# A write of ones moved behind the last causal masks of batch 0, and two copies of a transposed head moved from VectorE to ScalarE

## Chip, cores and metric

The kernel runs on one core of one Trainium2 chip. The metric is the device time of one execution in microseconds (us); of the kernel before there are three timed runs and one profiled execution. Engines go by the names of the profile: PE is TensorE (PEld its weight loads), DVE is VectorE, ACT is ScalarE, POOL is GpSimd, SP is SyncE, which here only issues DMAs.

## What is computed

Attention with a causal mask and a bias made of cumulative sums, over 8 batches of 8 heads (576 tokens, head size 64), then a mixer: a low-rank product over the tokens and a two-layer network over the 512 channels.

```python
s_pos = np.maximum(s, 0.0)
cum = np.cumsum(s_pos, axis=-1)
bias = -(cum[:, :, :, None] - cum[:, :, None, :])
scores = np.where(causal, -1e9, scale * q @ k.T + np.minimum(bias, 0.0))
attn = softmax(scores)
x = (attn @ v).transpose(0, 2, 1, 3).reshape(B, S, H * D)
u = x + (x.transpose(0, 2, 1) @ U @ V).transpose(0, 2, 1)
out = u + np.maximum(u @ w_ch1, 0.0) @ w_ch2
```

(`k.T` stands for the last two axes exchanged.)

## The kernel before

Heads are worked on in pairs: pair n = 4b + hp holds heads 2hp and 2hp + 1 of batch b, `hh` says which of the two. One pair passes through these steps:

- T(n), `transposes` (from L310): PE turns q and k so that the head size lies along the partitions (L325), for each `hh` into one PSUM bank `pwork`. Two copies for each `hh` (L348; `par` 0 and 1, even and odd tokens) bring them into the pair's `slot` in SBUF. `copies` (L296) says which engine copies: VectorE or ScalarE.
- The slot has four more rows (64 to 67) for the bias: `rows_of` (L303) brings two DMAs of cumulative sums from HBM, queued on SP; the other halves of these rows are ones. Slots 0 to 3 have their ones from batch 0's own rows. Slot 4, `slots[PB]`, first used by pair 4, gets them from the memset of L1169.
- S(n), `scores` (from L439): four steps, each a few matmuls (L443) into PSUM and an exponential on ScalarE into the tile `pT`: one for head 0 and one for head 1 (L461), one for the middle blocks of both (L473, "S6 mid" below for pair 6), and one for the last 64 tokens (L479, "S6 tail"), whose matmuls write a bank `pwork`. In batch 0 the causal masks are three `affine_select` instructions on GpSimd for each pair (`masks`, L391, by way of L158): head 0, head 1, and the last 64 tokens of both. From batch 1 on VectorE masks (L387).
- V(n), `values` (from L495): for each `hh` 15 matmuls (L507) into a bank `pwork`, then a reciprocal (L516) and a multiplication (L517) on VectorE, which frees the bank.

There are four banks `pwork`, given out and taken back as they fall free, and two double banks `pscore`. Around batch 0's end stand `mix_first` (M0 to M3, L621; its first half has the products of L625, its second those of L632 and L640 and a copy on ScalarE, L648) and the first blocks of the channel network's first layer, `hidden_first` (L677), which need the first half of `w_ch1` (`load_w1(0)`, 1 MB, issued by POOL at L1154). The second layer of batch 0's tokens starts with `ahead[0]` and `ahead[1]`: two banks `pwork`, begun by L688 and L696.

What sets the order: PE and POOL run in the order of the program (L1332), and up to L1205 DVE, ACT and SP do too. Behind that line a planner, which works with estimated durations, sets the order on DVE, ACT and SP, and which bank a tile gets. The order of steps is written out by hand. At batch 0's end on POOL it is: masks of pair 2, a small memset (L1167), the load of the second half of `w_ch1` (L1168), the memset of L1169, the masks of pair 3 (L1176), loads of q and k of batch 1 (L1177), of half of `w_ch2` (L1178). PE meanwhile goes S3, V1, M0, S3, V2, M0, M1, V3, M1, M2. In batch 1 the words around the moved copies are "S6 T7 S6 T7 S6 S6" and then "V4 V4 S7 V5" (L1247, L1248), with pieces of the channel network between them.

From batch 3 on, q and k are turned by DMA: `load_pair` loads a pair, `turn_pair` (L364) queues a DMA transpose on SP behind the last turned output of V (L524), and `part_pair` (L373) copies the result into the slot on VectorE (L377). `seqmix` (L531) mixes the tokens of a finished batch and begins with products over all its `x_sb` (L537).

Of the kernel before, what the change touches and what calls it, by code (L numbers as in the profile page):

```python
# [41 lines left out]
def kernel(  # L42
# [12 lines left out]
    nc = tc.nc  # L55
    traced = len(nc.cur_bb.bb.instructions)
    E = mybir.EngineType
    B, H, S, D = q.shape
# [8 lines left out]
    PB = NP // B  # L67
    TP, TT = 72, 8
    NG = B * S // 512
    KA = D + 4  # L70
# [46 lines left out]
    def in_runs(b, h):  # L117
        return b > 2 or b == 2 and h >= 4
# [10 lines left out]
    def load_qk(b, h, n):  # L129
        for dst, src in ((q_t[b], q), (k_t[b], k)):  # L130
            if in_runs(b, h):
                nc.gpsimd.dma_start(
                    out=dst[:, ds(h, n), :].rearrange("p h (t d) -> p (h t) d", t=TT),
                    in_=src[b, ds(h, n)].rearrange("h (t p) d -> p (h t) d", p=TP),
                )
            else:
                nc.gpsimd.dma_start(
                    out=dst[:, ds(h, n), :],
                    in_=src[b, ds(h, n)].rearrange("h (p t) d -> p h (t d)", p=TP),
                )  # L140
# [58 lines left out]
    slots = [consts.tile([128, 2, S + SK], BF16, name=f"slot{i}") for i in range(NSLOT)]  # L199
# [66 lines left out]
    def load_w1(half):  # L266
        nc.gpsimd.dma_start(
            out=w1_sb[:, :, ds(half * 1024, 1024)], in_=w1_in[:, :, ds(half * 1024, 1024)]
        )

    def load_w2(half):
        nc.gpsimd.dma_start(
            out=w2_sb[:, ds(half * 8, 8), :],
            in_=moe_w_ch2[ds(half * 1024, 1024)].rearrange("(kt kp) n -> kp kt n", kp=128),
        )
# [19 lines left out]

    def copies(n, hh, par):  # L296
        b = n // PB
        on_act = hh == (n == 4) and (
            n in (0, 4, 8, 9) or (n, par) == (1, 0) or n > 8 and n % PB == 2
        )  # L300
        return nc.scalar.copy if on_act else nc.vector.tensor_copy

# [7 lines left out]
    def transposes(n):  # L310
# [24 lines left out]
        for hh in range(2):  # L335
            if b > 0:
                turn(hh, 0)
            turn(hh, 1)
            tp = tps[hh]
            dst = slot[0:D, hh, 0 : 2 * S]  # L340
            for par in range(2):
                src = tp[par * D : par * D + D]
                if in_runs(b, 2 * hp):
                    by_run = dst.rearrange("p (c t two m) -> p c t two m", c=2, t=4, two=2)
                    copies(n, hh, par)(by_run[:, :, :, par, :], src)
                else:
                    in_turn = dst.rearrange("p (c m t two) -> p c m t two", c=2, t=4, two=2)
                    copies(n, hh, par)(  # L348
                        in_turn[:, :, :, :, par], src.rearrange("p c t m -> p c m t")
                    )  # L350
            yield
# [31 lines left out]
    def mask(dst, n_tiles, w, on_pool=False):  # L383
        if on_pool:
            causal(dst, n_tiles, w)
        else:
            nc.vector.tensor_tensor(  # L387
                dst, dst, keep[:, :, 0:w].to_broadcast([128, n_tiles, w]), op=ALU.min
            )

    def masks(pT, on_pool):  # L391
        for hh in range(2):
            mask(pT[:, hh, 0:512].rearrange("p (a b) -> p a b", a=4), 4, 128, on_pool)
        mask(pT[:, :, 1536:1600], 2, 64, on_pool)
# [726 lines left out]
    def pT_of(n):  # L1121
        if n < PB + 3:
            return pTs[n % 2] if n % PB < 2 else pT_early[n % PB - 2]
        return pTs[(n + 1) % 2]

    def step(*gens):
        for gen in gens:
            next(gen, None)
# [37 lines left out]
    masks(pT_of(2), True)  # L1166
    nc.gpsimd.memset(pT_early[1][:, :, 1600:], 1.0)  # L1167
    load_w1(1)  # L1168
    nc.gpsimd.memset(slots[PB][D:KA, :, 0 : 2 * S].bitcast(mybir.dt.uint32), 0x3F803F80)  # L1169
    step(S3)  # L1170
    step(V1)
    step(S3)
# [1 line left out]
    step(M0)  # L1174
    step(S3, S3)
    masks(pT_of(3), True)  # L1176
    load_qk(1, 4, 4)  # L1177
    load_w2(0)  # L1178
    nc.gpsimd.memset(V_end, 0.0)
# [183 lines left out]
```

## Time and profile before

| | |
|---|---|
| timed runs | 351.04 us median of 3 (350.96 to 352.51) |
| profiled execution | 351.77 us, of which the span of instructions is 349.9 us |
| granted TensorE clock | 1.00 |
| PE busy | 96% of the span |
| DVE, ACT, POOL busy | 75%, 59%, 34% |
| chain that ended last, by engine | PE 66%, DVE 12%, DMA 7%, POOL 6%, issue 4%, ACT 3% |
| idle time of PE in the list of its waits, 13 rows | 7.3 us |

The span is what the profile shows of the instructions; the rest of a run's time lies around it. The profile's lists of waits name for each engine whom it waited for, how long in total, how often, and the longest. A timeline line has start, duration, engine, line, operation, output<-input and form; "x3" means three merged instructions, and brackets hold the idle time before and what ended it. PE is busy nearly all the time, so a removed wait of PE can show in the end, if no later wait takes it back.

### The profile page before, as it was taken

To read this page: it belongs to the slowest core of one execution; us is meant where nothing else is said; L and a number is where in the kernel's file an instruction comes from. 1 tells how busy PE (TensorE), PEld (TensorE's weight loads), DVE (VectorE), ACT (ScalarE), POOL (GpSimd) and SP (SyncE) were. 2 spreads that over 40 slices of the span, in tenths; PEclk is the share of its full clock that TensorE was granted. 3 is DMA by queue.
4 is the path that set the end of the run, shared out by engine and by line. 5 is a ranking of instruction groups with operands and counts; after the bars stand their busy time and mean duration, and the time that the engine had idled before them with its cause. 6 is when DMAs were issued, how large, how long until landed. Compare 5 with 4: busy or idle time off the path is not lost.

```text
span 349.9 us, 9017 instructions
## 1 busy us (share of the span) xinstructions
PE 337.5 (96%) x3654; PEld 245.4 (70%) x3689; DVE 261.8 (75%) x579; ACT 205.6 (59%) x311; POOL 120.0 (34%) x173
## 2 busy tenths in 40 slices
PE   8989999999989999999999999999899999999996
PEld 3675656665578657875688568866587558888885
DVE  8885776778698747984699559965878588775774
ACT  4876975747843577347833784378561546675710
POOL 7997374671294348224553356000000000000000
PEclk9999999999999999999999999999999999999999
DMA  7999999999999999999999999584034335010022
GB/s 110 152 184 207 185 185 139 146 143 141 136 134 147 180 176 120 127 167 159 124 152 163 194 97 155 116 175 75 2 69 104 85 69 83 32 60 32 32 90 92
DMA packets 165601, 43.23 MB, mean 124 GB/s; under 512 B 150200, under 2 KB 163928, under 8 KB 165560
## 3 DMA queue, kind: packets, MB, share of 16 engines
q0 software_dynamic: 98896, 18.44, 72.5%
q1 hardware_dynamic: 66376, 24.01, 36.4%
q8 instruction: 29, 0.48, 0.6%
q10 hardware_dynamic: 288, 0.20, 0.2%
q14 instruction: 12, 0.10, 0.1%
HBM read 37.25 MB, written 9.70 MB: 134 GB/s over the span
## 4 chain that ended last, share of the span: by engine, by line
PE 66%; DVE 12%; DMA 7%; POOL 6%; issue 4%; ACT 3%; DVEq 0%; ACTq 0%; POOLq 0%
PE pwork L677 20%; PE pwork L735 12%; PE quarter L735 9%; PE pscore L443 7%; PE pwork L507 6%; PE parts L965 6%; DVE uT L562 2%; DMA qk_sd<-qk_sd 2%; DVE o_sb L749 2%; DVE slot L713 2%; DMA v_slot<-in_v_dram 2%; DMA qk_sd<-in_k_dram 2%; POOL v_slot L187 2%; PE pwork L696 1%; ACT pT L461 1%
## 5 line engine op out<-in xcount | busy, mean ns | idle before, releaser
L677 PE MATMUL pwork<-uT,w_sb 128*128 128x512 bf16 x406 | 104.1, 379 | 2.2 <-ACT hT L1054 0.9
L461 ACT ACTIVATE pT<-pscore 128x1024 bf16<-128x1024 f32 x57 | 57.6, 1029 | 50.9 <-PE pscore L443 50.7
L1054 ACT ACTIVATE hT<-pwork 128x512 bf16<-128x512 f32 x108 | 65.3, 610 | 35.4 <-PE pwork L677 34.5
L677 PEld LDWEIGHTS <-w_sb 128*128 128x128 bf16 x448 | 39.0, 98 | 38.1 <-issue 1.3
L443 PE MATMUL pscore<-slot 68*128 68x128 bf16 (+1 forms) x506 | 55.9, 246 | 0.5 <-DMA slot<-hT 0.3
L124 POOL DMA_DIRECT2D qk_sd<-in_q_dram x40 | 29.7, 743 | 76.7 <-DMA qk_sd<-qk_sd 39.6
L443 PEld LDWEIGHTS <-slot 68*128 68x128 bf16 x570 | 42.2, 97 | 18.2 <-issue 0.6
L735 PEld LDWEIGHTS <-hT 128*128 128x128 bf16 x496 | 46.8, 98 | 7.2 <-DVE uT L562 0.5
L387 DVE TENSOR_TENSOR pT<-pT,keep 128x512 bf16<-128x512 bf16 (+1 forms) x81 | 28.6, 354 | 28.6 <-ACT pT L461 22.6
L507 PEld LDWEIGHTS <-pT 128*128 128x128 bf16 x870 | 32.5, 98 | 6.7 <-issue 0.9
L507 PE MATMUL pwork<-v_slot,pT 128*128 128x65 bf16 x870 | 36.0, 193 | 1.1 <-DVE slot L348 0.6
L187 POOL DMA_DIRECT2D v_slot<-in_v_dram x40 | 34.2, 871 | 5.7 <-DMA w_sb<-in_moe_w_ch_dram 3.9
L517 DVE TENSOR_TENSOR x_sb<-pwork,rec 128x320 bf16<-128x320 f32 x64 | 31.1, 488 | 1.3
L473 ACT ACTIVATE pT<-pscore 128x1024 bf16<-128x1024 f32 x29 | 30.3, 1044 | 1.9 <-PE pscore L443 1.8
L124 POOL DMA_DIRECT2D qk_sd<-in_k_dram x40 | 29.7, 743 | 4.2 <-DMA qk_sd<-in_q_dram 2.5
L735 PE MATMUL pwork<-w_sb,hT 128*128 128x256 bf16 x240 | 29.9, 273 | 0.0
L348 DVE COPY slot<-pwork 64x576 bf16<-64x576 bf16 x31 | 24.9, 802 | 5.3 <-PE pwork L325 3.5
L735 PEld LDWEIGHTS <-slot 128*128 128x128 bf16 x256 | 24.1, 98 | 4.2 <-issue 1.2
L516 DVE RECIPROCAL rec<-pwork 128x5 f32<-128x5 f32 x64 | 12.1, 191 | 14.9 <-PE pwork L507 14.3
L735 PE MATMUL pwork<-w_sum,slot 128*128 128x256 bf16 x160 | 20.1, 272 | 0.4 <-DVE o_sb L749 0.4
L735 PE MATMUL quarter<-w_sb,hT 128*128 128x256 bf16 x144 | 18.0, 273 | 0.3 <-DVE uT L562 0.3
L978 DVE TENSOR_TENSOR hT<-pT,parts 128x512 bf16<-128x512 f32 x16 | 10.8, 685 | 6.3 <-PE parts L965 3.6
(167 smaller groups left out, 497.8 us busy)
## 6 DMA issues: line engine op xcount, KB each, us to landing
out_dram<-o_sb SPq DMA_DIRECT2D x34, 256.0 KB
v_slot<-in_v_dram POOLq DMA_DIRECT2D x32, 128.0 KB, 6.3
w_sb<-in_moe_w_ch_dram POOLq DMA_DIRECT2D x4, 1024.0 KB, 13.3
qk_sd<-in_q_dram POOLq DMA_DIRECT2D x40, 72.0 KB, 4.0
qk_sd<-in_k_dram POOLq DMA_DIRECT2D x40, 72.0 KB, 4.3
qk_sd<-in_q_dram POOLq DMA_DIRECT2D x4, 288.0 KB, 12.7
qk_sd<-in_k_dram POOLq DMA_DIRECT2D x4, 288.0 KB, 11.7
qk_sd<-in_q_dram POOLq DMA_DIRECT2D x4, 144.0 KB, 4.3
```

The costliest lines, as they stand in the source:

```text
L124: nc.gpsimd.dma_start(out=of_pair(n)[:, c, :, hh, :], in_=src[b, 2 * hp + hh].rearrange("(t p) d -> p t d", p=TR),)
L187: nc.gpsimd.dma_start(out=vt[:rows_t, t, :, 0:D], in_=v[b, :, ds(t * 128, rows_t), :].rearrange("h p d -> p h d"),)
L348: copies(n, hh, par)(in_turn[:, :, :, :, par], src.rearrange("p c t m -> p c m t"))
L387: nc.vector.tensor_tensor(dst, dst, keep[:, :, 0:w].to_broadcast([128, n_tiles, w]), op=ALU.min)
L443: nc.tensor.matmul(dst, lhsT=slot[0:KA, hh, ds(S + j * 128, 128)], rhs=slot[0:KA, hh, lo:hi], start=True, stop=True,)
L461: nc.scalar.activation(pT[:, hh, 0:1024], near, EXP, scale=scale)
L473: nc.scalar.activation(pT[:, :, 1024:1536], mid.rearrange("p (a b) -> p a b", a=2), EXP, scale=scale)
L507: nc.tensor.matmul(po[:, i, :], lhsT=pT[:, hh, ds(place(j, i), 128)], rhs=vt[:, j, h, :], start=(j == 0), stop=(j == i), skip_group_check= ...
L517: nc.vector.tensor_tensor(x_sb[:, hp, :, ds(hh * D, D)], po[:, :, 0:D], rec.to_broadcast([128, 5, D]), op=ALU.mult,)
L677: nc.tensor.matmul(f1, lhsT=w1_sb[:, kt, ds(nf * 128, 128)], rhs=u[:, kt, :], start=(kt == 0), stop=(kt == 3),)
L735: nc.tensor.matmul(acc[:, i, :], lhsT=a[:, kt, ds(i * 128, 128)], rhs=b[:, kt, :], start=(begin and i == 0 and kt == 0), stop=(kt == HF - ...
L1054: nc.scalar.activation(hT[:, nf, :], f1, RELU)
```

## The change

Two edits. In `copies`, pair 7 joins pair 4: the two copies of its head 1 (`hh` = 1, `par` 0 and 1) go to ScalarE; those of its head 0 stay on VectorE. And the memset of ones into slot 4 moves on GpSimd from ahead of S3's steps to just behind the masks of pair 3, ahead of the load of q and k.

```diff
     def copies(n, hh, par):
         b = n // PB
-        on_act = hh == (n == 4) and (
-            n in (0, 4, 8, 9) or (n, par) == (1, 0) or n > 8 and n % PB == 2
+        on_act = hh == (n in (4, 7)) and (
+            n in (0, 4, 7, 8, 9) or (n, par) == (1, 0) or n > 8 and n % PB == 2
         )
         return nc.scalar.copy if on_act else nc.vector.tensor_copy
...
     masks(pT_of(2), True)
     nc.gpsimd.memset(pT_early[1][:, :, 1600:], 1.0)
     load_w1(1)
-    nc.gpsimd.memset(slots[PB][D:KA, :, 0 : 2 * S].bitcast(mybir.dt.uint32), 0x3F803F80)
     step(S3)
     step(V1)
     step(S3)
     step(V1)
     step(M0)
     step(S3, S3)
     masks(pT_of(3), True)
+    nc.gpsimd.memset(slots[PB][D:KA, :, 0 : 2 * S].bitcast(mybir.dt.uint32), 0x3F803F80)
     load_qk(1, 4, 4)
     load_w2(0)
     nc.gpsimd.memset(V_end, 0.0)
```

## The prediction

> **What bounds the kernel now.** I read the page first, for the engines.
>
> ```profile
> PE 337.5 (96%) x3654; PEld 245.4 (70%) x3689; DVE 261.8 (75%) x579; ACT 205.6 (59%) x311; POOL 120.0 (34%) x173
> POOL 7997374671294348224553356000000000000000
> ```
>
> PE is busy throughout; POOL is full in the first slices (8.75 us each) only. Then the list of PE's waits, since a PE that hardly idles can be helped by little but its waits. Columns: total us, times, longest.
>
> ```profile
> PE pwork L537 <- DVE x_sb L517: 1.5, 1, 1.5
> ...
> PE pwork L507 <- POOL hT L158: 0.8, 2, 0.5
> PE pwork L507 <- DVE slot L348: 0.6, 1, 0.6
> ```
>
> All 13 rows add up to 7.3 us. The two edits are at rows two and three; row one lies downstream of both. Third, the timeline from 23 to 27 us:
>
> ```profile
> 23.04 1.05 POOL L1169 MEMSET slot<- 4x1152 uint32 x1
> ...
> 23.58 0.27 ACT L479 ACTIVATE hT<-pwork 128x128 bf16<-128x128 f32 x1
> ...
> 24.16 1.46 POOL L158 TENSOR_SCALAR_AFFINE_SELECT hT<-hT 128x512 bf16<-128x512 bf16 x3
> ...
> 25.68 0.73 PE L507 MATMUL pwork<-v_slot,hT 128*128 128x65 bf16 x18 [0.30 <-POOL hT L158]
> ...
> 26.96 0.38 PE L677 MATMUL pscore<-uT,w_sb 128*128 128x512 bf16 x1
> ```
>
> The memset stands between POOL's issue of `w_ch1` and the masks, while the masks' inputs are all but ready (the last exponential ends at 23.85); V3 on PE waits for masks twice (0.51 and 0.30 us). Fourth, the timelines of PE, DVE and ACT around 50 us, where T7's copies are:
>
> ```profile
> 50.01 1.61 DVE L348 COPY slot<-pwork 64x576 bf16<-64x576 bf16 x2
> ```
> ```profile
> 51.68 0.64 PE L507 MATMUL pwork<-v_slot,pT 128*128 128x65 bf16 x15 [0.56 <-DVE slot L348]
> 52.15 0.38 PE L688 MATMUL pwork<-ux_first,V_sb 128*128 128x512 bf16 x1
> ```
> ```profile
> 49.78 1.02 ACT L473 ACTIVATE hT<-pscore 128x1024 bf16<-128x1024 f32 x1 [0.76 <-PE pscore L443]
> 50.70 0.27 ACT L479 ACTIVATE hT<-pwork 128x128 bf16<-128x128 f32 x1
> 53.88 1.02 ACT L461 ACTIVATE pT<-pscore 128x1024 bf16<-128x1024 f32 x1 [2.90 <-PE pscore L443]
> ```
>
> The second half of V4 needs the bank that T7's last copy frees at 51.62. ACT is done with S6's head 1 at 49.02, and after S6 tail it has 2.9 us of idle time.
>
> **The memset, step by step.** The masks of pair 3 take POOL's place at 23.04 instead of 24.16, 1.12 us earlier. Their inputs allow it: head 0's and head 1's exponentials (two in 1.95 us from 20.69) end by 22.64, and the third mask would start near 24.2, after the tail exponential (23.85). They end at 23.04 + 1.46 = 24.50 instead of 25.62. PE is free for V3 when M0's and M1's products are issued, about 24.18 (five products of L625 from 23.90; 26.68 to 26.96 shows such five issued in 0.28). Twelve matmuls take 0.36, the remaining three then find the third mask done (24.56 with the 0.06 that PE needed after 25.62), and V3's end, now some 26.2, comes near 25.1: 1.1 us. Then something else is late next: the first block of L677 needs the first half of `w_ch1`, issued at 16.45.
>
> ```profile
> w_sb<-in_moe_w_ch_dram POOLq DMA_DIRECT2D x1, 1024.0 KB, 9.6
> ```
>
> It lands at 16.45 + 9.6 = 26.05, no earlier after the change. L677's weight load starts at 26.91 now and could start at 26.08: **0.83 us** gained. Bounds: 0.5 (the first wait alone) to 1.12 (the landing comes earlier too).
>
> The memset itself goes to 24.50 to 25.56, so the loads behind it keep 25.58: nothing there. Queued behind it on SP are the two `rows_of` DMAs for slot 4, issued at 24.12 and 24.40 right behind the memset, the last before 45.98; they go to about 25.6, and S4 reads slot 4 at 34.92, or 34.1 then. Eight us cover it; without that cover the price would be the shift, 1.5. Data that PE, now earlier, will ask for: q and k of batch 1 (issued at 19.94, 8.6 us to land, so 28.5; T4 at 31.8, then 31.0), second set (26.30 + 10.8 = 37.1; T6 at 40.9, then 40.0), half of `w_ch2` (26.99 + 14.8 = 41.8; L696 at 48.3). All stay ahead.
>
> **The copies.** On DVE two copies of 64x576 go, 1.61 us. On ACT two come: the same form there, from 59.49, took 1.62 for two. With S6's head 1 done at 49.02 and T7's transposes issued by 48.1, ACT copies from 49.02 to 50.64; V4's second half can start when PE is done with the first half, 50.51 + 0.45 = 50.96, not 51.68. That is 0.72 gross. But ACT is in order, and S6 mid and S6 tail stand behind the copies: S6 mid 50.6 to 51.55, tail until 51.8 instead of 50.97. Who waits for that: VectorE's mask of S6 tail (51.52 now), the reciprocals of V4 behind it, and `ahead[1]` (L688). Of four banks one is held by `ahead[0]`, two by V4's halves (first freed at 52.48), so L688, which started at 52.15, must have had S6 tail's bank. It now waits for it until about 51.85: **0.30 us** earlier than now. Bounds: 0.72 if the planner finds another free bank, and -0.6 if it gives L688 the bank of V4's first half, which the later mask frees near 52.7. I take 0.30: the same bank as now. The next exponential on ACT (53.88) has idle time to spare.
>
> The Trainium skill ("VectorE: DVE Perf Modes", the errata section) speaks against the move: its cycle table gives a bf16 copy from PSUM (120 + 576/2)/0.96 GHz, an estimate of 425 ns, on VectorE, and (172 + 576)/1.2 GHz, 623 ns, on ScalarE. By it VectorE would be done at about 50.9, the move would bring nothing, and the sum would be 0.83. The trace disagrees: L348 took 800 ns on VectorE and 798 on ScalarE (medians).
>
> **Sum and what is left of it.** 0.83 + 0.30 = 1.13 us by 52 us. Then the way to 104 us:
>
> ```profile
> 95.91 0.92 DVE L377 COPY slot<-qk_sd 64x1152 bf16<-64x1152 bf16 x2 [0.89 <-DMA qk_sd<-qk_sd]
> ```
>
> DVE waits there for DMA transposes that SP issued at 89.08, then is full until its normalising at 102.82, and PE's one long wait (1.48, at 103.76) is for that. PE's gain stays only if those transposes come earlier too. SP issued them 0.18 after the transpose of x (87.67 to 88.90), which went 0.03 after its input on DVE: they follow PE's and DVE's progress. But they take 6.7 us to land beside loads, with DMA busy at nine tenths in every slice from 9 to 218 us. I keep four fifths, 0.9. After 105 us the chain is mostly PE. Span 349.9 - 0.9 = 349.0; the median lies 1.14 above the profiled span, so **350.1 us**, own range 349.4 to 350.8.
>
> **Rivals.**
>
> *Absorbed.* The transposes land at 95.8 whatever PE does, DVE's queue stays, and PE only waits longer at 103.76, 1.48 + 1.1. For it: the full DMAs. Against: SP's issue times above. Of the 1.13 some 0.1 is left: 350.9.
>
> *A new order on VectorE, slower.* The planner orders DVE anew once 1.6 us of its work are gone. The place is the products of a finished batch (L537), which seven batches have and only one shows with such a wait. At 103.76 the order cost 1.48, because sums of L713 (0.61 each in sequence) stood ahead of the normalising. If one more batch falls so, 1.48 - 0.9 is lost: 351.6; if two, 2.06: 353.1. It decides from 0.9 us of new waits. Against: the order now gives one such place in seven.
>
> *A new order, faster.* The same freedom the other way: the normalising at 102.82 goes ahead of two or three sums, and the wait of 1.48 falls away on top of the 0.9: 348.7.
>
> *The edit of the copies does nothing* (another releaser than the trace infers): 0.83 at most, four fifths kept, 350.4, inside the forecast's range.
>
> **Chances.** The forecast, with the copies' null case, 0.42; absorbed 0.14; slower 0.24, of which 0.08 with one place and 0.16 with two; faster order 0.20. What a measurement of this kernel can tell from no change is about 0.5%, 1.76 us: the bounds are 349.28 and 352.80. Under 349.28 lie the faster order and 0.04 of the forecast: 0.24. Above 352.80 lie the two places and 0.02 of mishaps unnamed: 0.18. Within: 0.58. The range must reach both sides: from 348.5, just under the faster order, to 352.9, leaving out the two places and little else; the likeliest case alone has 349.4 to 350.8.
>
> **What would show it.** After: no wait of L507 for POOL near 25 us, masks of pair 3 on POOL from about 23.04, L677 first at about 26.1 with a short wait for `w_ch1`; ACT with two copies L348 ending near 49.8 (50.64 less the first 0.83), no wait of V4's second half, L688 near 51.0. Wrong would be: the masks still starting near 24.1, for want of their inputs; L688 later than 52; PE's wait near 103 grown by 1 us (absorbed); or new waits of PE for `x_sb` after 110 us (new order).

## The result, and the profile after

The changed kernel took 350.21 us in the median of 22 runs (349.51 to 351.14), the kernel before 351.17 in 22 runs beside it (350.51 to 352.51): ratio 0.9969, 95% interval 0.996 to 0.9978, or 1.1 us less (0.96 by the medians). The profiled execution took 350.08 us, with a span of 348.4 against 349.9.

The page of the changed kernel, span and busy time of each engine:

```profile
span 348.4 us, 9017 instructions
...
PE 337.0 (97%) x3654; PEld 245.2 (70%) x3689; DVE 260.2 (75%) x577; ACT 207.1 (59%) x313; POOL 120.4 (35%) x173
```

PE does the same work in a shorter span; two copies (1.6 us on DVE) have gone from DVE to ACT. The changed kernel's list of PE's waits (total us, times, longest):

```profile
PE pscore L443 <- DMA slot<-hT: 0.8, 2, 0.6
PE pscore L582 <- DVE ux L552: 0.7, 2, 0.6
PE pwork L537 <- DVE x_sb L517: 0.7, 1, 0.7
...
PE pwork L688 <- ACT hT L479: 0.2, 1, 0.2
```

The rows for GpSimd's masks (0.8) and for VectorE's copy of the slot (0.6) are gone. The row of L537 has halved, which neither edit touches; the experiments come back to it. New is L688's wait for ScalarE's last exponential of pair 6. Other rows grew: L443's wait for the bias rows from 0.3 to 0.8 and L507's for `v` from 0.3 to 0.5, both before 20 us and so ahead of either edit, and L582's from 0.3 to 0.7. All rows together went from 7.3 to 6.2 us. The changed kernel's timeline at the memset:

```profile
23.05 1.59 POOL L158 TENSOR_SCALAR_AFFINE_SELECT hT<-hT 128x512 bf16<-128x512 bf16 x3
...
24.60 1.08 PE L507 MATMUL pwork<-v_slot,hT 128*128 128x65 bf16 x30
24.69 1.05 POOL L1176 MEMSET slot<- 4x1152 uint32 x1
...
25.69 0.72 POOL L137 DMA_DIRECT2D qk_sd<-in_q_dram  x1
...
26.23 1.03 PE L677 MATMUL pscore<-uT,w_sb 128*128 128x512 bf16 x4
```

V3's 30 matmuls run through without a wait, L677's matmuls start at 26.23 and not 26.96, and the load of q that follows the memset is where it was (25.58 before). And at the copies, ScalarE and then PE of the changed kernel:

```profile
47.27 1.02 ACT L461 ACTIVATE hT<-pscore 128x1024 bf16<-128x1024 f32 x1
48.19 1.61 ACT L348 COPY slot<-pwork 64x576 bf16<-64x576 bf16 x2
49.83 1.02 ACT L473 ACTIVATE hT<-pscore 128x1024 bf16<-128x1024 f32 x1
50.75 0.27 ACT L479 ACTIVATE hT<-pwork 128x128 bf16<-128x128 f32 x1
```
```profile
49.77 1.08 PE L507 MATMUL pwork<-v_slot,pT 128*128 128x65 bf16 x30
51.07 0.38 PE L688 MATMUL pwork<-ux_first,V_sb 128*128 128x512 bf16 x1 [0.21 <-ACT hT L479]
```

V4's two halves follow each other without a pause; L688 then waits until S6 tail is out of its bank (50.75 + 0.27 = 51.02), 1.08 us earlier than the 52.15 of before.

Instruction by instruction, the planner's new order differs from the old one in little: PE and SP are the same, POOL and ACT differ by the moved instructions alone, and DVE by these and by seven small copies of `V_sb` (L1244, L1245) that now alternate.

### The profile page after: what moved, and what is told of

Same layout as the page of the kernel before. It is cut to its first block, busy times and chain, and to the rows that moved or that the text cites. A ratio compares the mean times of both kernels' runs of the same rounds, so it can differ in the third digit from the quotient of the medians.

```text
span 348.4 us, 9017 instructions
## 1 busy us (share of the span) xinstructions
PE 337.0 (97%) x3654; PEld 245.2 (70%) x3689; DVE 260.2 (75%) x577; ACT 207.1 (59%) x313; POOL 120.4 (35%) x173
## 4 chain that ended last, share of the span: by engine, by line
PE 73%; DVE 12%; ACT 4%; issue 4%; DMA 4%; POOL 1%; SPq 1%; DVEq 0%; ACTq 0%
PE pwork L677 21%; PE pwork L735 12%; PE quarter L735 10%; PE pscore L443 8%; PE pwork L507 7%; PE parts L965 6%; PE pwork L696 3%; DVE uT L562 2%; DVE slot L713 2%; DMA v_slot<-in_v_dram 2%; DMA qk_sd<-qk_sd 2%; ACT hT L1054 2%; ACT pT L461 1%; DVE o_sb L749 1%; PE pwork L965 1%
## 5 line engine op out<-in xcount | busy, mean ns | idle before, releaser
L677 PE MATMUL pwork<-uT,w_sb 128*128 128x512 bf16 x406 | 104.1, 379 | 2.2 <-ACT hT L1054 0.9
L677 PEld LDWEIGHTS <-w_sb 128*128 128x128 bf16 x448 | 39.0, 98 | 38.1 <-issue 1.3
L443 PE MATMUL pscore<-slot 68*128 68x128 bf16 (+1 forms) x506 | 55.9, 245 | 0.9 <-DMA slot<-hT 0.8
L443 PEld LDWEIGHTS <-slot 68*128 68x128 bf16 x570 | 42.1, 97 | 19.1 <-issue 1.3
L507 PEld LDWEIGHTS <-pT 128*128 128x128 bf16 x870 | 32.5, 98 | 6.1 <-issue 0.9
L507 PE MATMUL pwork<-v_slot,pT 128*128 128x65 bf16 x870 | 35.9, 193 | 0.8 <-DMA v_slot<-in_v_dram 0.5
L348 DVE COPY slot<-pwork 64x576 bf16<-64x576 bf16 x29 | 23.3, 803 | 4.7 <-PE pwork L325 3.2
```

Source lines behind the costliest of these rows:

```text
L443: nc.tensor.matmul(dst, lhsT=slot[0:KA, hh, ds(S + j * 128, 128)], rhs=slot[0:KA, hh, lo:hi], start=True, stop=True,)
L507: nc.tensor.matmul(po[:, i, :], lhsT=pT[:, hh, ds(place(j, i), 128)], rhs=vt[:, j, h, :], start=(j == 0), stop=(j == i), skip_group_check= ...
L677: nc.tensor.matmul(f1, lhsT=w1_sb[:, kt, ds(nf * 128, 128)], rhs=u[:, kt, :], start=(kt == 0), stop=(kt == 3),)
```

## The experiments

The theory: the masks bring about 0.8 us and the copies 0.3, and most of it reaches the end. The rival that came nearest to it: DMA transposes near 90 us land when they land, and take the gain back.

**The masks alone, and the memset twice.** The first kernel keeps the memset's new place and undoes the copies:

```diff
-        on_act = hh == (n in (4, 7)) and (
-            n in (0, 4, 7, 8, 9) or (n, par) == (1, 0) or n > 8 and n % PB == 2
+        on_act = hh == (n == 4) and (
+            n in (0, 4, 8, 9) or (n, par) == (1, 0) or n > 8 and n % PB == 2
         )
```

> The memset edit alone; T7's copies stay on VectorE. If the two waits of PE for GpSimd's masks are worth 1.1 us at V3 and PE keeps this to the end (the theory): no wait of L507 for POOL, the wait of V4's second half for VectorE still 0.5 to 0.6 us, and 0.8 to 1.1 us less than before (ratio 0.997 to 0.9977). If the DMA transposes near 90 us take the gain back (absorbed): PE's wait at the products L537 grows by 1 us, and at most 0.2 us is left. If the copies made the gain: no change.

350.55 us (12 runs) against 351.25: ratio 0.9974, interval 0.9959 to 0.9989, so 0.9 us less, as the theory expected. V4's wait of 0.6 for VectorE is back, and L537's wait was 1.7, hardly more than the 1.5 of before. The second kernel is the one before with the suspected cost doubled:

```diff
     nc.gpsimd.memset(slots[PB][D:KA, :, 0 : 2 * S].bitcast(mybir.dt.uint32), 0x3F803F80)
+    nc.gpsimd.memset(slots[PB][D:KA, :, 0 : 2 * S].bitcast(mybir.dt.uint32), 0x3F803F80)
```

> The kernel before with the memset of ones issued twice ahead of the masks of pair 3, so that the suspected cost is doubled. Theory: the masks start 1.05 us later, V3 on PE waits 1.05 us longer, and the end comes 0.8 to 1.1 us later than before (ratio 1.0023 to 1.003). Absorbed: PE's wait at L537 near 104 us shrinks by as much, and the end moves by 0.2 us at most.

352.57 us: ratio 1.0027, interval 1.0009 to 1.0044, so by the ratio 0.95 us slower for one more memset (1.3 by the medians). Its timeline on POOL and on PE:

```profile
22.97 1.05 POOL L1169 MEMSET slot<- 4x1152 uint32 x1
24.08 1.05 POOL L1170 MEMSET slot<- 4x1152 uint32 x1
25.21 1.47 POOL L158 TENSOR_SCALAR_AFFINE_SELECT hT<-hT 128x512 bf16<-128x512 bf16 x3
```
```profile
25.90 0.54 PE L507 MATMUL pwork<-v_slot,hT 128*128 128x65 bf16 x12 [1.22 <-POOL hT L158]
26.73 0.73 PE L507 MATMUL pwork<-v_slot,hT 128*128 128x65 bf16 x18 [0.30 <-POOL hT L158]
```

The masks come 1.05 us later and PE with them, by the whole of it. In this one profile L537 then waited 0.42, not 1.48, and started at 103.78 against 103.76: just what "absorbed" expected there. The timed runs decide against it, since one profile's wait is a sample, as shown below. Taken away (twice, the second time below) or added, a memset in this place is worth 0.6 to 1.0 us by the ratios, where "absorbed" expected 0.2 at most; the three intervals are each about half a microsecond wide on either side, and one of them reaches down to 0.1.

**The copies alone.** The kernel before with the new `copies`.

> The move of the two copies alone; the memset stays ahead of the masks. Theory: V4's second half no longer waits (0.72 us earlier), L688 waits some 0.2 us for S6 tail's bank, 0.3 to 0.4 us are left at 52 us and 0.3 us at the end (ratio 0.999, at the edge of what can be told). If ScalarE's queue were the costly part: no gain or a loss of 0.3. If the copies made most of the gain: 0.8 us or more.

V4's wait is gone, L688 waits 0.21 for ScalarE as in the changed kernel, and PE is 0.34 us ahead there (the table below). The time was 351.25 against 351.25, ratio 1.0 with an interval of 0.998 to 1.002: the 0.3 us that were expected are 0.001 and can't be told from nothing in it. Its profiled execution shows the waits for the masks with 0.3 where there were 0.8 before, since PE was itself 0.7 us later at V2 in that execution.

**One copy of the two.** To take the remaining wait of L688 away, only `par` 1 went to ScalarE:

```diff
-            n in (0, 4, 7, 8, 9) or (n, par) == (1, 0) or n > 8 and n % PB == 2
+            n in (0, 4, 8, 9) or (n, par) in ((1, 0), (7, 1)) or n > 8 and n % PB == 2
```

> The changed kernel, but only one of the two copies of T7's head 1 goes to ScalarE (par 1); par 0 stays on VectorE, so the two run side by side. Theory (L688's wait is ScalarE's queue, with S6 mid and S6 tail behind two copies): ScalarE is free 0.8 us earlier, the bank of T7's head 1 is freed in time all the same, neither V4 nor L688 waits, and PE is 0.3 us further ahead at 52 us than in the changed kernel; the end 0.2 to 0.4 us below it. Rival (the one copy left on VectorE, behind the mask, frees the bank too late): V4's second half waits again some 0.1 to 0.3 us and nothing is gained over the changed kernel.

The rival's outcome, but not by its mechanism, and with a longer wait than its 0.1 to 0.3 us. ScalarE, then VectorE, then PE of this kernel:

```profile
48.88 1.02 ACT L473 ACTIVATE hT<-pscore 128x1024 bf16<-128x1024 f32 x1 [0.76 <-PE pscore L443]
49.96 0.80 ACT L348 COPY slot<-pwork 64x576 bf16<-64x576 bf16 x1
50.78 0.28 ACT L479 ACTIVATE hT<-pwork 128x128 bf16<-128x128 f32 x1
```
```profile
49.12 0.80 DVE L348 COPY slot<-pwork 64x576 bf16<-64x576 bf16 x1
```
```profile
50.80 0.62 PE L507 MATMUL pwork<-v_slot,pT 128*128 128x65 bf16 x15 [0.58 <-ACT slot L348]
```

I had expected the two copies side by side. ScalarE's starts at 49.96, just when VectorE's ends (49.92) and when ScalarE is through with S6 mid (49.90), which the planner put ahead of it: they run one after the other, and this row alone does not say for which of the two reasons. The bank is freed at 50.76 and V4 waits 0.58 again. Every kernel here has such a pair of copies at the start: of T1's head 0, `par` 0 is on ScalarE and `par` 1 on VectorE. In the kernel before, ScalarE's runs from 10.33 to 11.11 and VectorE's starts at 11.15, after an idle time of 1.25 us that ended with ScalarE's copy. So the program makes the two copies of one head wait for each other. T0's copies, two from one bank on ScalarE (6.94 to 8.56) and two from another bank into the other head's half of the slot on VectorE (7.24 to 8.85), overlap. Whether the shared bank or the interleaved columns is the reason was not separated. Time 350.82, ratio 0.9986 (0.9964 to 1.0008): no gain over the changed kernel.

**The kernel before, the changed one and the masks, again.** Three more profiles, the last two timed on one chip.

> The kernel before, profiled once more. If PE's wait at the products L537 near 104 us is set by when the DMA transposes land, which moves from execution to execution, it may be anywhere from 0.4 to 1.7 us here (1.5 in the first profile, 1.7 with the masks alone, 0.4 with the memset twice). If it is a fixed part of the kernel before, it is 1.4 to 1.6 again. The two waits for GpSimd's masks (0.8 together) and V4's wait (0.6) should be there as before.

> The changed kernel again, for a second profile and beside the masks alone on one chip. Both edits: 0.9 to 1.2 us less than before. If the copies bring 0.3 us, it lies 0.3 us below the masks alone; if the copies' gain at 52 us is lost later, the two are equal. L688's wait for ScalarE's tail again 0.2 us, no wait of V4.

> The memset edit alone, again, beside the changed kernel on one chip: 0.8 to 1.0 us less than before. V4's wait of 0.6 us for VectorE is there again.

The kernel before (351.74 us, one run) showed 0.9 at L537, not 1.5, with nothing changed. Its waits for the masks were 0.3 in one place, not 0.8 in two as expected, since PE came to V2 0.4 us later. The changed kernel took 350.20 (ratio 0.9977, 0.996 to 0.9993), 0.8 us less than before by the ratio, with 1.5 there; the masks alone 350.73 (0.9984, 0.9973 to 0.9996), by the ratio 0.6 us less than before and not the 0.8 to 1.0 expected. The difference between these two, 0.5 us by the medians and 0.25 by the ratios, has the expected sign, and their intervals overlap. The profiles together, from the timelines (us from the start of the span):

| kernel | first weight load of V2 (L507) | weight load of M1's second half (L632) | first weight load of L677 | half of `w_ch1` lands | L688 of `ahead[1]` | L688 less L677 | wait at L537 |
|---|---|---|---|---|---|---|---|
| before | 22.49 | 26.21 | 26.91 | 26.03 | 52.15 | 25.24 | 1.48 |
| before, again | 22.88 | 26.21 | 26.91 | 24.66 | 52.15 | 25.24 | 0.92 |
| memset twice | 22.82 | 27.27 | 27.96 | 24.95 | 53.21 | 25.25 | 0.42 |
| copies alone | 23.17 | 26.29 | 26.98 | 24.66 | 51.88 | 24.90 | 0.54 |
| masks alone | 22.70 | 25.27 | 25.97 | 24.50 | 51.22 | 25.25 | 1.65 |
| masks alone, again | 22.52 | 25.15 | 26.51 | 26.47 | 51.73 | 25.22 | 0.72 |
| changed | 22.91 | 25.49 | 26.18 | 24.95 | 51.07 | 24.89 | 0.73 |
| changed, again | 22.49 | 25.07 | 26.08 | 26.04 | 50.94 | 24.86 | 1.49 |
| changed, third | 22.62 | 25.20 | 25.89 | 24.97 | 50.80 | 24.91 | 0.89 |

Read by column. With one memset ahead of the masks, M1's second half stands at 26.21 to 26.29 whatever came before; it is set by POOL. With the masks first it moves between 25.07 and 25.49: 0.7 to 1.1 us earlier. There it follows PE's own progress, 2.57 to 2.63 us behind V2's first weight load, and V2 starts at 22.49 in one execution and at 22.91 in another. With the memset first, such a late start is hidden behind POOL (the same distance is 3.12 to 4.45 us); with the masks first it counts. So the gain is largest where PE comes early, as in the profile that the prediction read. L677 follows M1's second half by 0.69 to 0.70, except in the two profiles with the masks first in which `w_ch1` lands after 26.0. The list of waits of the masks alone, second profile, names it:

```profile
PE pscore L677 <- DMA w_sb<-in_moe_w_ch_dram: 0.5, 1, 0.5
```

From L677 to L688 PE takes 25.22 to 25.25 us where VectorE copies, and 24.86 to 24.91 where ScalarE does: 0.35 us on average. The last column goes with neither edit.

**What sets the wait at L537.** DVE's row at the transposes' landing, in the second profile of the changed kernel (wait 1.49 at L537) and in that with the memset twice (0.42):

```profile
94.69 0.92 DVE L377 COPY slot<-qk_sd 64x1152 bf16<-64x1152 bf16 x2 [0.90 <-DMA qk_sd<-qk_sd]
```
```profile
95.99 1.09 DVE L377 COPY slot<-qk_sd 64x1152 bf16<-64x1152 bf16 x2
```

SP issued these transposes at 87.86 in the one and 90.14 in the other, behind the transposes of x, as the prediction read it. They landed 6.8 us later in the first (94.69) and at most 5.85 in the second, where DVE waited for nothing. The two profiles of the kernel before show it with nothing else changed: SP issued at 89.08 in both, the transposes landed at 95.91 and at 95.34, and L537 waited 1.48 and 0.92. So PE's early gain does bring the transposes forward, but their landing moves by a microsecond from execution to execution, and DVE, which has sums (L713) queued behind it and the normalising behind these, hands that on to PE. All nine profiles of the table agree ("none" is a wait too short for the list):

| kernel | wait of VectorE (L377) for the transposes | wait of PE at L537 | span, less the start of L688, less the wait at L537 |
|---|---|---|---|
| before | 0.89 | 1.48 | 296.3 |
| before, again | 0.34 | 0.92 | 296.9 |
| memset twice | none | 0.42 | 296.7 |
| copies alone | none | 0.54 | 296.4 |
| masks alone | 1.10 | 1.65 | 296.6 |
| masks alone, again | 0.39 | 0.72 | 296.7 |
| changed | 0.24 | 0.73 | 296.6 |
| changed, again | 0.90 | 1.49 | 296.5 |
| changed, third | 0.40 | 0.89 | 296.3 |

PE's wait is 0.3 to 0.6 us longer than VectorE's, whatever the kernel. Without the wait at L537 the way from L688 to the end is the same within 0.6 us, and with it it differs by 1.4 (296.9 to 298.3): what PE waits at L537 reaches the end almost whole. The wait is 1.10 us on average in the five profiles with the masks first and 0.84 in the four others; a loss of 0.26 is small beside the spread, so these profiles can't tell whether a part of the early gain is lost here.

A test of the queue: the changed kernel with four of these sums pinned to their place in the program, so that the planner puts them behind the normalising.

```diff
             product(p2, A12, B21, i)
-            total(A_3, A11, A21, ALU.subtract, i)
+            (placed if g == 1 else (lambda f: f()))(lambda: total(A_3, A11, A21, ALU.subtract, i))
...
             product(p6, A_2, B_2, i)
-            total(A_4, A12, A_2, ALU.subtract, i)
+            (placed if g == 1 else (lambda f: f()))(lambda: total(A_4, A12, A_2, ALU.subtract, i))
```

> The changed kernel, with four sums of L713 for token group 1 (two into hT, two into A_4) pinned to their place in the program, so that the planner no longer puts them ahead of the normalising at 101 us. If VectorE's queue behind the landing sets PE's wait at L537: the wait (0.7 in the changed kernel's profile) is gone or under 0.2, the normalising comes some 2 us earlier, and the end is 0.4 to 0.8 us below the changed kernel's (about 349.6). If the wait only moves to the next step (uxT behind a copy that waits for a transpose): a new wait of PE at L550 or L582, and no gain.

> The kernel of e6 again, since it had five runs only. If its wait only moved from L537 to L582, it equals the changed kernel in executions with a short wait at L537 and gains where that wait would be 1.5: 0.2 to 0.5 us below the changed kernel's median on the same chip.

L537 no longer waits; the products' last five start 0.85 us earlier than in the changed kernel's first profile, and this row of PE comes up instead:

```profile
106.28 0.39 PE L582 MATMUL pscore<-V_sb,ux 32*128 32x512 bf16 x2 [0.83 <-DVE ux L552]
```

L582 of the changed kernel's first profile started at 106.26, so all of it was given back within 5 us: the cast of `ux` now stands behind the moved sums. Times 349.64 (5 runs, ratio 0.9958, 0.9943 to 0.9973) and 349.83 (8 runs, 0.9954, 0.9936 to 0.9971): 349.79 over both, against 350.09 over the changed kernel's 46 runs in three comparisons. Beside the first of them, on the same chip, the changed kernel took 350.20, 0.56 us more; beside the second it took as little, where 0.2 to 0.5 us more was expected. So the two are not told apart:

> The changed kernel once more, beside the two on one chip: 0.8 to 1.1 us less than before, L537's wait anywhere from 0.4 to 1.7 us.

349.84, ratio 0.9964 (0.9944 to 0.9984), by the ratio 1.3 us less than before. The last kernel moved two of the sums further back in the program, behind the products of A_1 and B_1; those of A_4 stay pinned:

```diff
-            total(A_3, A11, A21, ALU.subtract, i)
+            g > 1 and total(A_3, A11, A21, ALU.subtract, i)
...
-            product(p5, A_1, B_1, i)
+            product(p5, A_1, B_1, i); g == 1 and placed(lambda: total(A_3, A11, A21, ALU.subtract, i))
```

> The changed kernel with the sums of token group 1 placed later still: the two of A_4 pinned as in e6, and the two into hT moved in the program behind the next products (A_1 by B_1) and pinned there. In e6 PE's wait at L537 went, and 0.83 us of wait for ux came at L582, behind two of these sums and a late cast. If the wait there is VectorE's queue, ux comes 1.2 us earlier, neither L537 nor L582 waits over 0.3 us, and the end is 0.5 to 0.9 us below the changed kernel's on the same chip. If VectorE's whole load up to 110 us is the bound, the wait moves on once more, to L607 or to the next scores, and the two are within 0.3 us.

350.27, ratio 0.9966 (0.9951 to 0.9981): no better than the changed kernel, against 0.5 to 0.9 us expected. The waits of PE in it are spread over three places:

```profile
105.91 0.39 PE L582 MATMUL pscore<-V_sb,ux 32*128 32x512 bf16 x2 [0.66 <-DVE ux L552]
109.69 1.03 PE L735 MATMUL pwork<-w_sb,hT 128*128 128x256 bf16 x8 [0.30 <-DVE o_sb L749]
110.96 0.62 PE L507 MATMUL pwork<-v_slot,pT 128*128 128x65 bf16 x15 [0.23 <-DVE uT L562]
```

In both orders that were tried the wait moved on. PE reached this last row's matmuls (L507) at 110.58 to 110.96 in their three profiles, and at 110.56 to 111.29 in the changed kernel's three, latest where L537 had waited 1.49: against the shorter draws nothing was gained by 111 us. That VectorE's work as a whole bounds PE from the landing near 94 us to there fits this, but was not shown: VectorE is busy 14.7 to 15.2 of the 17 us from 94 to 111 in these kernels, and in the changed kernel's first profile it idles for 1.48 us before 104.64.

## Why the prediction was right

The forecast was 350.1 us, the time 350.21, within the range and on the side that was named. That they agree to 0.1 us is in part luck: 0.9 us were taken off a median of three runs, 351.04, while 22 runs beside the changed kernel gave 351.17 (the 1.14 between median and profiled span only carries that median over; the profiled execution itself lies 1.9 above its span); and the sum was read from one profile whose waits are samples. By its steps:

- **The masks.** V3's end was to come 1.1 us earlier; M1's second half, which follows it, came 0.7 to 1.1 earlier in five profiles with this edit, and the masks started at 23.00 to 23.09 (23.04 foretold). The 1.1 holds where PE comes to V2 as early as in the profile that was read (22.49). The term of 0.83 for L677 took a cap from one landing of `w_ch1`, 26.05. In all profiles the landing lies between 24.50 and 26.47; the cap held in two of the five profiles above with the masks first (gains at L677 of 0.83 and 0.40, the latter under the bound of 0.5) and was absent in three (0.73 to 1.02). Their mean is 0.78: the size was right, but as a mean over a landing that moves, not as the fixed edge that the prediction made of it.
- **The loads and S4 behind the memset.** The load of q went from 25.58 to 25.69, the `rows_of` DMAs of slot 4 to 25.77, and no wait of S4 came of it.
- **The copies.** Gross 0.72, of which L688 gives back part by waiting for S6 tail's bank: foretold 0.30 net, measured 0.35; foretold "until about 51.85", measured 51.88 with the copies alone and ScalarE named (51.07 in the changed kernel). The prediction set the cycle table of the Trainium skill ("VectorE: DVE Perf Modes", the errata section) against the move, with the factor Accel of its VectorE row at 2: by that estimate of 425 ns a copy the move would bring nothing. For these copies that did not hold: L348 took 0.80 us on either engine (1.61 for two on ScalarE). With Accel at 1 the same row gives an estimate of 725 ns, which is nearer. The traces show that the order of the elements matters: L348 reads its bank out of order and writes to every second element, while the copies of L345, of the same size, read in order and write in runs; they took 454 ns on VectorE and 634 on ScalarE (medians). Whether the reading or the writing costs the rest was not separated. Whether the 0.35 us reaches the end stays open: 0.0 alone, and by the ratios about 0.2 in both comparisons of the changed kernel with the masks alone, all within the intervals.
- **The rest of the way.** Four fifths were kept as a guess from the profile of one execution (whose transposes took 6.8 us to land by the rows shown, not 6.7). The memset experiments agree with it (0.91 and 0.56 us for the masks alone by their ratios, 0.95 for the added memset, for steps of about 0.8 and 1.05), but their intervals are too wide to tell four fifths from all or from half. What was mistaken was to treat the wait of 1.48 at L537 as the kernel's own: the same kernel showed 0.92 the second time. The rivals that put a price of 1.48 on it, the two new orders above all, took a draw for a constant, and pinning the order (the faster rival tried directly) brought 0.56 us in one comparison and nothing in the other, not 1.48.
- **The planner.** It could have reordered VectorE's later work in either direction; apart from the moved copies it changed the places of seven small copies.

## What to carry to other kernels

An instruction that nobody needs soon, on an in-order engine ahead of ones that PE waits for, can cost PE up to its full length even if that engine is only a third busy: the added memset of 1.05 us cost 1.06 at M1, and taking it away gave 0.7 to 1.1, by how early PE came. Look at what stands just ahead of a releaser in its own queue. When a copy moves to another engine, cost the instructions that it pushes back there and the buffers they hold: here half of the 0.72 us gained went to the next bank. And profile the same kernel twice before building on a single wait: one that hangs on a DMA's landing is a sample.

## What was not expected of the hardware

The 1 MB load of half of `w_ch1`, issued at 16.33 to 16.49 us in all executions, landed 8.1 to 10.0 us later. The DMA transposes, issued at 89.08 in both profiles of the kernel before, landed 6.8 and 6.3 us later, and at most 5.85 later with the memset twice; with the sums queued behind them this moves PE's wait at one place between 0.42 and 1.65 us over nine profiles. And copies of 64x576 elements out of PSUM took 0.80 us on VectorE and on ScalarE where they read out of order and wrote to every second element (L348), but 0.45 and 0.63 where they read in order and wrote in runs (L345).
